# Rebuilding the instruction order of a one-core Conformer block: slack for GpSimd's results, shared last stores, and norm scaling of the tail on VectorE

## The chip, the cores and the metric

One core of a Trainium2 chip. The metric is the device time of one execution in microseconds (us), the median of the fast executions. The kernel before takes 951.6 us (three executions, 951.39 to 951.72). The profile of an execution covers a span about 1.8 us shorter than its time (949.6 for 951.43 before).

In this kernel TensorE (PE) multiplies matrices, VectorE (DVE) and ScalarE (ACT) work elementwise, GpSimd (POOL) takes the norms' powers and scalings and the edge copies, and SP issues most of the DMAs. "Clock" below is the share of full speed that TensorE was granted.

## The reference, cut to what matters

```python
B, T, D, K, H = 2, 4000, 144, 5, 4
h = layernorm(x);  x = x + 0.5 * (silu(h @ w_ff1a) @ w_ff1b)
h = layernorm(x);  q, k, v = split(h @ w_qkv)            # 4 heads of 36
x = x + softmax(q @ k.T * 36**-0.5) @ v @ w_o            # 4000 x 4000 scores a head
h = layernorm(x);  a, b = split(h @ w_pw1);  h = a * sigmoid(b)
c = depthwise_conv(h, dw)                                # 5 taps along T, zero padded
x = x + silu(c) @ w_pw2
h = layernorm(x);  x = x + 0.5 * (silu(h @ w_ff2a) @ w_ff2b)
return layernorm(x)
```

The 8000 tokens are handled as 16 chunks of 500. A chunk's convolution needs edge columns of its neighbours.

## The kernel before

The program is not written down in order. A scheduler runs while the kernel is built: threads (feed-forward, projections, attention, convolution of each chunk) ask for an engine and buffers, and a model with assumed costs decides whose instruction comes next. What it records is then replayed, with semaphores put in from the recorded reads and writes. So the chip runs a fixed order; if a result is later than the model assumed, an engine waits in that order (TensorE for 2.22 us at one place of the kernel before).

Model and records, cut:

```python
LAT = dict(pe=0.165, act=0.12, dve=0.083, pool=0.1, sp=2.0)     # us from an instruction's end to its result
def op(self, eng, name, *a, r=(), w=(), q=None, cost=0.1, kind=None, lat=None, **k):
    ...                                  # dependences from the keys in r and w
    self.free[eng] = o.t1 = start + cost
    o.done = start + cost + ((self.LAT[eng] if q is None else 2.0) if lat is None else lat)
```

Layer norm: VectorE takes the statistics, GpSimd the power -0.5. In the middle of the kernel GpSimd also scales; in the tail ACT or VectorE does:

```python
if not calm:                                              # the middle: GpSimd
    for j in range(n):
        op("pool", "tensor_scalar", XN[..., u, j, :], X[...], RS[..., 2, j], RS[..., 0, j], ..., cost=XN_COST, lat=XN_LAT)
elif mode["tail"] and R.free["act"] + XSLACK < R.free["dve"]:   # the tail, when ACT is free earlier
    op("dve", "scalar_tensor_tensor", ...)                # -mean * rstd
    for j in range(n):
        op("act", "activation", XN[...], X[...], ACT.Identity, bias=..., scale=..., cost=c_act(D))
else:
    for j in range(n):
        op("dve", "tensor_scalar", XN[...], X[...], ST[...], RS[...], ..., cost=0.231)
```

The edges of the convolution. U1 holds the gated values of 128 channels, U2 those of the other 16. Both copies write under one key, "UL", and the convolution over U1 reads that key:

```python
op("pool", "tensor_copy", U1[:, u, 2:4, 0:1], U1[:, up, 2:4, TB:TB + 1], r=[("U", up)], w=[("UL", u)], cost=0.25)
op("pool", "tensor_copy", U2[0:LP, u, 0:1], U2[0:LP, up, TB:TB + 1], r=[("V", up)], w=[("UL", u)], cost=0.25)
...
op("pe", "matmul", o[:, i0:i1, :], lhsT=DG[:, tap, :], rhs=U1[...], r=[("U", u), ("UL", u), ("UR", u), "DG"], w=[("ps", bk)], ...)
```

The softmax here doesn't subtract the row's maximum and nothing guards it: scores larger than these inputs give would overflow.

## Time and profile before

| stretch of the span (us) | length | ACT busy | ACT idle | VectorE busy |
|---|---|---|---|---|
| start, 0 to 139 | 139.0 | 121.8 | 17.2 | 121.2 |
| middle, 139 to the last exponential at 911.7 | 772.7 | 754.7 | 18.0 | 713.1 |
| tail, from there to the end | 37.9 | 23.4 | 14.5 | 21.6 |

ACT is the engine to watch: 804.0 of its 899.8 busy us are exponentials, and it is busy for 754.7 of the middle's 772.7 us, so an idle ACT there is counted as lost time. In the tail there are no exponentials, and the length is that of a chain of short steps on all engines. In lines of the trace a bracket holds the idle time just before an instruction and what ended it.

### The profile page before, as it was taken

How to read it: one execution, taken by the hardware profiler on the slowest of the kernel's cores; microseconds unless marked ns; L12 is line 12 of the kernel's file. 1: busy time of each engine (PE TensorE's matmuls, PEld its weight loads, DVE VectorE, ACT ScalarE, POOL GpSimd, SP SyncE). 2: the span in 40 equal slices, each digit the busy share in tenths (PEclk: the TensorE clock that was granted, in tenths of full speed). 3: DMA queues.
4: the chain of work that ended last, by engine and by line, in shares of the span. 5: the costliest groups of instructions: out<-in, count | busy, mean ns of one | idle time of the engine just before them, and what ended most of it. 6: DMA issues, size and time to landing. Idle time of an engine off the chain costs nothing.

```text
span 949.6 us, 26625 instructions
## 1 busy us (share of the span) xinstructions
PE 892.5 (94%) x11433; PEld 406.3 (43%) x11433; DVE 855.9 (90%) x1881; ACT 899.8 (95%) x1153; POOL 303.1 (32%) x524
## 2 busy tenths in 40 slices
PE   8999999999989999999999999999999999999996
PEld 6543434334444334444444343443444443434455
DVE  7998889999969999999899999999999998985874
ACT  5799998999979999999999999999999999999976
POOL 4130142410615215051322540232414343334052
PEclk9999999999989999999999999999999999999998
DMA  4000000000000000000000000000000000000000
GB/s 121 22 2 2 1 2 2 2 1 1 3 1 2 2 2 1 2 1 2 2 7 2 14 2 2 1 7 9 1 8 1 9 7 1 8 8 9 1 8 25
DMA packets 7321, 7.30 MB, mean 8 GB/s; under 512 B 2377, under 2 KB 7204, under 8 KB 7204
## 3 DMA queue, kind: packets, MB, share of 16 engines
q1 hardware_dynamic: 6046, 5.14, 1.8%
q8 instruction: 89, 1.46, 0.7%
q10 hardware_dynamic: 1158, 0.48, 0.2%
q14 instruction: 28, 0.23, 0.1%
HBM read 3.31 MB, written 2.30 MB: 6 GB/s over the span
## 4 chain that ended last, share of the span: by engine, by line
ACT 55%; PE 34%; DVE 8%; issue 1%; DMA 0%; POOL 0%; DVEq 0%
ACT PT L169 49%; PE PS L169 34%; ACT TH L169 5%; DVE PT L169 4%; DVE HT L169 1%; DVE ST L169 1%; ACT XN L169 1%; DVE X L169 1%; DMA X<-in_x_dram 0%; DVE XT L169 0%; DVE OTF L169 0%; DVE U L169 0%; ACT HT L169 0%; POOL U L169 0%; DVE XN L169 0%
## 5 line engine op out<-in xcount | busy, mean ns | idle before, releaser
L169 ACT ACTIVATE PT<-PS 128x1000 bf16<-128x1000 f32 (+1 forms) x869 | 804.0, 1046 | 16.1 <-PE PS L169 14.2
L169 PE MATMUL PS<-QT,KT 64*64 64x500 bf16 x3968 | 411.7, 385 | 27.8 <-ACT PT L169 20.2
L169 PE MATMUL PS<-PT,VA 64*37 64x500 bf16 x3968 | 361.0, 376 | 5.6 <-DVE OTF L169 2.7
L169 PEld LDWEIGHTS PS<-QT,KT 64*64 64x64 bf16 x3968 | 123.7, 104 | 221.6 <-ACT PT L169 144.3
L169 DVE TENSOR_SCALAR PT<-PS 128x500 uint16<-128x500 f32 x278 | 186.0, 670 | 15.4 <-PE PS L169 14.7
L169 DVE TENSOR_TENSOR PT<-PT 128x1000 f16<-128x1000 f16 (+1 forms) x278 | 187.6, 680 | 2.3
L169 POOL TENSOR_SCALAR RS<-ST 125x4 f32<-125x4 f32 x114 | 39.1, 343 | 427.3 <-DVE ST L169 421.7
L169 DVE TENSOR_SCALAR PT<-PT 128x1000 uint16<-128x1000 uint16 (+1 forms) x417 | 167.4, 417 | 2.6
L169 PEld LDWEIGHTS PS<-PT,VA 64*37 64x37 bf16 x3968 | 116.0, 95 | 116.9 <-issue 27.8
L169 POOL TENSOR_SCALAR XN<-X,RS 125x144 bf16<-125x144 bf16 x228 | 143.9, 643 | 5.9
L169 POOL TENSOR_TENSOR RS<-RS,NHALF 125x4 f32<-125x4 f32 (+2 forms) x101 | 99.5, 989 | 102.8 <-DVE RS L169 97.8
L169 ACT ACTIVATE TH<-PS 128x500 bf16<-128x500 f32 (+2 forms) x201 | 108.4, 562 | 8.4 <-PE PS L169 7.9
L169 DVE SCALAR_TENSOR_TENSOR HT<-TH,PS 128x500 bf16<-128x500 bf16 (+1 forms) x140 | 83.8, 615 | 12.9 <-ACT TH L169 12.7
L169 PE MATMUL PS<-XT,WA 72*128 72x500 bf16 (+2 forms) x280 | 73.8, 360 | 1.8 <-DVE HT L169 0.5
L169 DVE SCALAR_TENSOR_TENSOR X<-PS,X 125x288 bf16<-125x288 f32 x128 | 57.4, 452 | 10.7 <-PE PS L169 8.9
L169 DVE BATCH_NORM_STATS2 ST<-X 125x6 f32<-125x288 bf16 (+1 forms) x160 | 65.5, 447 | 1.4 <-DMA X<-in_x_dram 1.2
L169 PE MATMUL PS<-WB,HT 128*125 128x144 bf16 (+1 forms) x640 | 52.3, 230 | 1.7 <-DVE HT L169 1.4
L169 PEld LDWEIGHTS PS<-WB,HT 128*125 128x125 bf16 (+1 forms) x640 | 44.4, 136 | 15.5 <-issue 4.6
L169 POOL COPY U<-U 128x2 bf16<-128x2 bf16 (+1 forms) x54 | 17.1, 343 | 103.4 <-DVE U L169 103.4
L169 DVE COPY XT<-PS 72x1000 bf16<-72x1000 bf16 (+1 forms) x66 | 40.7, 617 | 7.6 <-PE PS L169 6.9
L169 PE MATMUL PS<-IDENT,XN 125*72 125x125 bf16 x512 | 42.6, 222 | 2.7 <-DVE XN L169 1.4
L169 PEld LDWEIGHTS PS<-IDENT,XN 125*72 125x72 bf16 x512 | 31.3, 113 | 23.2 <-issue 11.7
(88 smaller groups left out, 602.2 us busy)
## 6 DMA issues: line engine op xcount, KB each, us to landing
X<-in_x_dram SPq DMA_DIRECT2D x16, 140.6 KB
out_dram<-XN SPq DMA_DIRECT2D x13, 140.6 KB
out_dram<-XN SPq DMA_DIRECT2D x4, 70.3 KB
WA<-in_w_ff1a_dram ACTq DMA_DIRECT2D x1, 144.0 KB
WB<-in_w_ff1b_dram ACTq DMA_DIRECT2D x1, 144.0 KB, 2.7
WA<-in_w_ff2a_dram SPq DMA_DIRECT2D x1, 144.0 KB
WB<-in_w_ff2b_dram SPq DMA_DIRECT2D x1, 144.0 KB
out_dram<-XN SPq DMA_DIRECT2D x1, 139.5 KB
```

The costliest lines, as they stand in the source:

```text
L169: ins = getattr(eng, o.name)(*o.a, **o.k)
```

## The change

The policy tables are constants for each stage of the attention. DSLACK, for example, sets how far behind TensorE VectorE may be and still take a tile of exponentials off ACT.

The change's intent: leave room in the model for GpSimd's results, by assuming them later (norm scaling 0.1 to 0.6 us, edge copies 0.1 to 0.8); have the convolution ask for its edges before it is placed; retune the policy tables to the new model; in the tail, tell the model that a block scaled on ACT costs 0.41 us and prefer VectorE; let ACT issue some of the last stores.

```diff
-    BASE = dict(AHEAD=0.56, DSLACK=0.2, ..., BMIN=2.0, ...)
+    BASE = dict(AHEAD=0.56, DSLACK=0.4, ..., BMIN=1.6, ...)
     POLICY = {
-        "DSLACK": [0.2, 0.2, 0.2, 0.2, 0.2, 0.2, 0.2, 1.0, 1.0, 0.6, 0.2, ...],
+        "DSLACK": [0.4, 0.4, 1.5, 1.5, 1.5, 1.5, 1.5, 0.6, 1.0, 0.6, 0.4, ...],
  ... (DGAP, BMIN, SOON, EARLY retuned; LATE added; FDVE 4 to 5, PRELAG 0.5 to 0.7)
-                   ... w=[("XN", u)], cost=c_act(D))
+                   ... w=[("XN", u)], cost=0.41)
-    XSLACK = 0.0
+    XSLACK = 0.5
-    XN_LAT = 0.1
+    XN_LAT = 0.6
  ... (the four edge copies:)
-               cost=0.25)
+               cost=0.25, lat=0.8)
  ... (in post2, before the convolution's threads start:)
+        S.cur.ready = max([S.cur.ready] + [R.ready((k, c % NU), "pe") for k in ("U", "V", "UL", "UR")[:2 if e else 4]])
-        def put(dst, src, u, eng="sp"):
-            op(eng, "dma_start", dst, src, q=q, r=[("XN", u)], cost=0.7)
+        def put(dst, src, u):
+            act = mode["tail"] and R.free["act"] < R.free["sp"]
+            op("act" if act else "sp", "dma_start", dst, src, q=q, r=[("XN", u)], cost=0.4 if act else 0.7)
```

More of the change, by code (lines that the diff above doesn't have):

```diff
@@ L355, in bass_standalone__conformer_family_zipformer__speech_kernel @@
     NAN = 5
-    BASE = dict(AHEAD=0.56, DSLACK=0.2, DGAP=4.0, OFREE=1, OBATCH=1, LATE=0.3, BMIN=2.0, SOON=2, LIVE=3, MAXQ=3, EARLY=2)
+    BASE = dict(AHEAD=0.56, DSLACK=0.4, DGAP=4.0, OFREE=1, OBATCH=1, LATE=0.3, BMIN=1.6, SOON=2, LIVE=3, MAXQ=3, EARLY=2)
     POLICY = {
-        "DSLACK": [0.2, 0.2, 0.2, 0.2, 0.2, 0.2, 0.2, 1.0, 1.0, 0.6, 0.2, 0.2, 0.2, 0.2, 0.2, 0.2, 0.2, 0.2],
-        "DGAP": [4.0, 4.0, 4.0, 4.0, 4.0, 4.0, 4.0, 4.0, 4.0, 4.0, 4.0, 4.0, 4.5, 4.5, 4.0, 4.0, 4.0, 4.0],
+        "DSLACK": [0.4, 0.4, 1.5, 1.5, 1.5, 1.5, 1.5, 0.6, 1.0, 0.6, 0.4, 0.4, 0.4, 0.4, 0.4, 0.4, 0.4, 0.4],
+        "DGAP": [4.0, 4.0, 4.0, 4.0, 4.0, 4.0, 4.0, 4.0, 4.0, 4.5, 4.5, 4.5, 4.5, 4.5, 4.0, 4.0, 4.0, 3.5],
         "OFREE": [1, 1, 1, 1, 1, 1, 1, 1, 1, 1, 1, 3, 1, 3, 0, 0, 0, 1],
         "OBATCH": [1, 1, 1, 1, 1, 1, 1, 1, 1, 1, 1, 1, 1, 0, 1, 1, 1, 2],
-        "BMIN": [2.0, 2.0, 2.0, 2.0, 1.8, 1.8, 1.8, 2.0, 2.0, 1.6, 2.0, 3.5, 2.0, 2.0, 2.0, 2.0, 2.0, 1.8],
-        "SOON": [2, 2, 2, 2, 2, 2, 2, 2, 2, 2, 2, 2, 2, 2, 2, 2, 5, 3],
+        "LATE": [0.3, 0.3, 0.3, 0.1, 0.1, 0.3, 0.3, 0.3, 0.3, 0.3, 0.3, 0.3, 0.3, 0.3, 0.3, 0.3, 0.3, 0.3],
+        "BMIN": [1.6, 1.6, 1.6, 1.6, 1.8, 1.6, 1.8, 1.6, 1.6, 1.6, 1.6, 3.5, 3.5, 1.6, 1.6, 1.6, 1.6, 1.8],
+        "SOON": [2, 2, 2, 2, 2, 2, 2, 2, 2, 2, 2, 2, 2, 4, 4, 2, 5, 3],
         "LIVE": [3, 2, 2, 2, 3, 3, 3, 3, 3, 2, 2, 3, 3, 3, 2, 3, 3, 3],
         "MAXQ": [3, 3, 3, 3, 3, 3, 3, 3, 2, 2, 2, 2, 2, 3, 3, 3, 3, 3],
-        "EARLY": [2, 2, 2, 2, 2, 2, 2, 1, 1, 1, 1, 1, 1, 2, 2, 2, 2, 2],
+        "EARLY": [2, 2, 2, 2, 2, 2, 2, 1, 1, 2, 2, 2, 2, 2, 2, 2, 2, 2],
     }
@@ L376, in bass_standalone__conformer_family_zipformer__speech_kernel @@
     NQ = 2
-    FDVE = 4
+    FDVE = 5
     FEQ = 2
     HALF = 5
-    PRELAG = 0.5
+    PRELAG = 0.7
     BEND = 2.0
@@ L621, in ln @@
                    bias=RS[0:rows, u, 2, j:j + 1], scale=RS[0:rows, u, 0, j:j + 1],
-                   r=[("X", c, b0 + j), ("NM", u), ("RS", u)] + xe, w=[("XN", u)], cost=c_act(D))
+                   r=[("X", c, b0 + j), ("NM", u), ("RS", u)] + xe, w=[("XN", u)], cost=0.41)
         else:
@@ L966, in halo @@
             op("pool", "tensor_copy", U1[:, u, 2:4, 0:1], U1[:, up, 2:4, TB:TB + 1], r=[("U", up)], w=[("UL", u)],
-               cost=0.25)
+               cost=0.25, lat=0.8)
             op("pool", "tensor_copy", U2[0:LP, u, 0:1], U2[0:LP, up, TB:TB + 1], r=[("V", up)], w=[("UL", u)],
-               cost=0.25)
+               cost=0.25, lat=0.8)
         if cc == CPB - 1 or c == NCH - 2:
@@ L1017, in post1 @@
             op("pool", "tensor_copy", U1[:, up, 0:2, TB + 1:TB + 2], U1[:, u, 0:2, 1:2], r=[("U", u)],
-               w=[("UR", up)], cost=0.25)
+               w=[("UR", up)], cost=0.25, lat=0.8)
             op("pool", "tensor_copy", U2[0:LP, up, TB + 1:TB + 2], U2[0:LP, u, 1:2], r=[("V", u)], w=[("UR", up)],
-               cost=0.25)
+               cost=0.25, lat=0.8)
         glu_done.add(c)
@@ L1138, in store @@
             if e and 3 in bs:
-                put(out_tok[c - 1][TB - 1:TB, 2:4, :], XN[TB:TB + 1, u, 0:2, :], u, "act")
+                put(out_tok[c - 1][TB - 1:TB, 2:4, :], XN[TB:TB + 1, u, 0:2, :], u)
             xnp.give(u)
```

## The prediction

> **What bounds the kernel now.** I read the page from the top: busy shares first, then the chain that ended last, then the groups, then waits and timelines of the places that stood out.
>
> ```profile
> PE 892.5 (94%) x11433; PEld 406.3 (43%) x11433; DVE 855.9 (90%) x1881; ACT 899.8 (95%) x1153; POOL 303.1 (32%) x524
> ...
> PEclk9999999999989999999999999999999999999998
> ...
> ACT 55%; PE 34%; DVE 8%; issue 1%; DMA 0%; POOL 0%; DVEq 0%
> ...
> L169 ACT ACTIVATE PT<-PS 128x1000 bf16<-128x1000 f32 (+1 forms) x869 | 804.0, 1046 | 16.1 <-PE PS L169 14.2
> ```
>
> ACT is busy for 95% of the span and the chain runs mostly on it: the exponentials of the attention scores are 804 of its 899.8 us. So time can only be won in three ways: less work for ACT, fewer holes in ACT's row, or a shorter end after the last exponential. The clock row has one digit that is not 9 in the middle, and that is the first thing to chase. To place holes I cut the span at two points: 139, where the two programs stop being the same (below), and 911.7, where ACT's last exponential ends. The sums by stretch, in the order PE, weight loads, DVE, ACT, POOL:
>
> ```profile
> 0.00:139.00 139.00, 132.26 (x1680) 65.67 (x1680) 121.23 (x335) 121.75 (x171) 39.47 (x70) 1.00 0.09 26
> 139.00:911.70 772.70, 733.19 (x9426) 317.93 (x9424) 713.14 (x1476) 754.71 (x930) 253.12 (x436) 1.00 0.02 4
> 911.70:949.60 37.90, 27.10 (x333) 22.70 (x330) 21.57 (x73) 23.38 (x55) 10.50 (x20) 0.92 0.06 16
> ```
>
> In the middle ACT is idle for 772.7 - 754.7 = 18.0 us. The narrower stretch 264 to 284 has 12.99 us of ACT busy in 20.00, so 7.0 of the 18.0 us lie in that one place. Its timeline and the windows of 2 us around it:
>
> ```profile
> 264.97 1.25 DVE L169 TENSOR_TENSOR PT<-PT 128x1000 uint16<-128x1000 uint16 x2
> 266.14 0.74 DVE L169 TENSOR_SCALAR PT<-PT 128x1000 uint16<-128x1000 uint16 x2
> ```
>
> ```profile
> 264.52 2.66 POOL L169 COPY U<-U 80x1 bf16<-80x1 bf16 x3 [2.03 <-DVE U L169]
> ...
> 266.98 0.39 PE L169 MATMUL PS<-U,DG 128*128 128x500 bf16 x1 [2.22 <-POOL U L169]
> ```
>
> ```profile
> 268.00:270.00 2.00, 2.00 (x10) 0.56 (x8) 0.00 (x0) 1.81 (x2) 0.00 (x0) 0.50 0.00 0
> 270.00:272.00 2.00, 2.00 (x13) 0.54 (x13) 0.00 (x0) 1.58 (x2) 0.00 (x0) 0.50 0.00 0
> 272.00:274.00 2.00, 2.00 (x21) 1.06 (x23) 0.87 (x2) 0.75 (x2) 0.00 (x0) 0.50 0.00 0
> ```
>
> The convolution's first matmul waits 2.22 us for edge columns that GpSimd copies. A copy of one column usually takes about 0.19 us (median of the 54 such copies, 187 ns); the first of these three took 2.41 us and ended at 266.93, just after DVE's run of work (264.38 to 266.88) ended. Then TensorE's clock stands at half for 6.8 us (267.5 to 274.4), so scores come late and ACT starves until about 282. One late 80x1 copy costs 7 us.
>
> [...] In this trace a store's issue is about 0.27 us on SP, so sharing stores can save a few tenths.
>
> **The change, part by part.** This kernel decides its order while it is built, from assumed costs. The change makes GpSimd's results appear later in that model (norm scaling 0.1 to 0.6, edge copies to 0.8), makes the convolution ask for its edges before it is placed, retunes the policy tables, makes ACT's norm scaling in the tail look dearer, and lets ACT issue stores in the tail. Comparing the two built programs:
>
> First, the start is the same: up to TensorE instruction 1680, ACT 179, VectorE 336. In the trace TensorE's lies at 139.0 us, so the 139 us stay.
>
> Second, ACT's work in the middle: 2 fewer 1000-column exponentials (2 x 1.054 = 2.1 us less), 2 more 500-column tanh (2 x 0.645) and one small one (0.29), together 0.5 us less: 754.2. VectorE gets two more attention tiles (about 4.0 us each from the rows: 2 x 0.67, 3 x 0.417, 2 x 0.68) and some feed-forward and convolution products, about 9 us more: 722. In some 765 us that is 94%, below ACT's 98.6%.
>
> Third, the edge stall. I counted the TensorE columns that stand between the last left-over GLU matmul (the one that the U edge depends on) and the next convolution. Before, the smallest distance is 9,000 columns, and it is exactly the stall at 267; the next, 14,000 and 17,000, did not stall. After, the smallest is 21,000. So I expect no convolution to wait for GpSimd by over half a microsecond, and no half clock in the middle: 7.0 us won, all on the path, as ACT is the bound.
>
> Fourth, the other 11.0 us of ACT holes. The largest is 2.49 us at 162.87, where TensorE runs about 18,000 columns of other work within 8 score matmuls. The new order has such a place too (about 21,800 columns), and otherwise similar densities. I give the new order 10 us of holes, so 8.0 us won of 18.0.
>
> Fifth, the tail, 37.9 us, a chain in which ACT is busy only 23.4. Norm scaling on ACT falls from 22 blocks to 10, on VectorE it rises from 6 to 22. A block costs 0.50 on ACT and 0.31 on VectorE, and ACT's form needs a further 0.15 us VectorE instruction. The last stretch is clearest:
>
> ```profile
> 942.56 0.69 POOL L169 TENSOR_TENSOR RS<-RS,NHALF 126x2 f32<-126x2 f32 x1 [0.37 <-DVE RS L169]
> 942.58 3.29 ACT L169 ACTIVATE XN<-X,RS 125x144 bf16<-125x144 bf16 x8 [0.90 <-DVE RS L169]
> 943.29 0.16 DVE L169 SCALAR_TENSOR_TENSOR RS<-ST,RS 126x2 f32<-126x2 f32 x1 [0.67 <-POOL RS L169]
> ```
>
> The last power ends at 943.25, but ten scalings queue on ACT until 945.87. With the last two on VectorE (0.6 us) that point is near 943.9: 2.0 us won. The two earlier norms of the last chunk win about 0.5 each. Fewer feed-forward tiles with tanh and one whole convolution are also left after the last exponential (three fewer VectorE products of 0.67 us, 15 fewer convolution matmuls), and a second issuer saves about 0.3. Overlaps eat some of this; I take 3.5 us in all.
>
> Sum: 951.6 - 0.5 - 8.0 - 3.5 = **939.6 us**, 1.3% less.
>
> **Rivals.** (a) The bound moves to VectorE: its middle rises to 94%[...] and TensorE waits elsewhere. For it: the early chunks' policy now allows many more tiles. Against it: only 2 tiles more in all, and waits of TensorE for GpSimd's norm output were 1.4 us in total before. It would take back 3 to 6 us: 943 to 946. (b) Order noise: a rebuilt order makes a new hole like the one at 162.87 or, if TensorE stands for 2 us, another half-clock stretch of 7 us; the cluster of 21,800 columns is the candidate. Then 944 to 948. (c) The order is better everywhere: holes fall to 5 us and the tail to 33: about 933. With no holes at all in the middle and a tail of 34.4, 139 + 754.2 + 34.4 and 1.8 us of difference between time and span give 929.4, so a gain over 2% (below 932.6) needs holes below about 3 us. (d) Stores bound the end, so the shorter chain gains nothing: against it, the last packet lands 2.6 us after the last issue and the queue is nearly empty before.
>
> **Range and chances.** The two sure terms (edge stall, last scalings) give 9 us. The rest is order luck of about 6 us either way: 933 to 947. Over 2% faster is barely above the floor: 0.07. Over 2% slower would need 30 us of new holes: 0.01. Within 2%: 0.92.
>
> **What would show it.** Right: the clock row is whole in the middle, no TensorE wait for POOL U over 0.5 us, ACT's busy total near 893, ACT idle in the middle near 10, the span after the last exponential near 34.5. Wrong: a second half-clock stretch, a new wait of TensorE for POOL XN or of ACT for scores over 3 us, VectorE waits vanishing at a busy share above 96% in the middle, or a tail as long as before although scaling moved.

The 0.3 us for a second issuer, within the 3.5, is the estimate from what a store's issue takes on SP in the trace of before (median 0.26 us of 19, 0.25 to 0.32); the "2 us" and "7 us" of rival (b) are this trace's one case, 2.22 us of waiting with 6.8 us of half clock.

## The result, and the profile after

The changed kernel takes 938.9 us (four executions, 938.82 to 939.81) against 951.5 us for the kernel before on the same chip. The ratio is 0.9874, 95% interval 0.9856 to 0.9891: a gain clear of noise, and within the 2% that counts as "same". A ratio here is the mean time of one kernel's fast executions over that of the other's of the same rounds, so not quite the ratio of the medians quoted. Executions over 1.5% slower than the fastest of the same kernel are left out of the means.

The page after, in the order of the lines shown of before: busy time, clock by slice, the chain, the exponentials' group.

```profile
PE 891.4 (95%) x11427; PEld 405.4 (43%) x11427; DVE 864.1 (92%) x1905; ACT 893.2 (95%) x1141; POOL 291.9 (31%) x518
...
PEclk9999999999999999999999999999999999999999
...
ACT 50%; PE 32%; DVE 14%; POOL 2%; issue 1%; DMA 0%; POOLq 0%; DVEq 0%
...
L169 ACT ACTIVATE PT<-PS 128x1000 bf16<-128x1000 f32 (+1 forms) x867 | 801.7, 1046 | 13.8 <-PE PS L169 12.4
```

ACT works 6.6 us less, and no slice of the clock falls below 9. The sums by stretch (length, then busy time of PE, weight loads, DVE, ACT, POOL; clock; DMA), cut at the same two events:

```profile
0.00:139.00 139.00, 133.07 (x1679) 66.51 (x1679) 121.19 (x334) 121.73 (x171) 39.45 (x70) 1.00 0.09 26
139.00:904.66 765.66, 733.56 (x9430) 316.89 (x9428) 719.07 (x1490) 752.67 (x930) 242.26 (x431) 1.00 0.01 4
904.66:937.02 32.36, 24.75 (x324) 21.96 (x321) 23.80 (x82) 18.85 (x41) 10.22 (x17) 0.97 0.08 24
```

The start is the same. The middle is 7.0 us shorter: 2.0 by less work on ACT, 5.0 by less idling (18.0 to 13.0). The tail is 5.5 us shorter. TensorE's waits in the middle, totals with count and longest:

```profile
PE PS L169 <- ACT PT L169: 20.8, 51, 0.8
PE PS L169 <- POOL XN L169: 1.6, 2, 1.1
PE PS L169 <- DVE OTF L169: 1.4, 3, 0.8
```

The wait for POOL U is gone. Two small waits for GpSimd's norms (POOL XN) are new. The largest hole on ACT is now the 2.46 us that end at 433.73, behind a dense group of other matmuls:

```profile
431.00 0.27 ACT L169 ACTIVATE TH<-PS 80x125 bf16<-80x125 f32 x1 [1.34 <-PE PS L169]
...
433.73 2.90 ACT L169 ACTIVATE PT<-PS 128x1000 bf16<-128x1000 f32 x3 [2.46 <-PE PS L169]
```

The end of the tail: the last power on GpSimd ends at 933.29, VectorE scales the last blocks until 933.87, and two stores go out on each of SP and ACT.

```profile
931.93 1.36 POOL L169 TENSOR_TENSOR RS<-RS,NHALF 126x2 f32<-126x2 f32 x2 [0.73 <-DVE RS L169]
932.24 0.17 DVE L169 TENSOR_SCALAR RS<-ST 125x2 f32<-125x2 f32 x1
932.66 1.21 DVE L169 TENSOR_SCALAR XN<-X,ST,RS 126x144 bf16<-126x144 bf16 x4 [0.25 <-POOL RS L169]
932.67 0.79 SPq L169 DMA_DIRECT2D out_dram<-XN  x2
933.24 0.95 ACTq L169 DMA_DIRECT2D out_dram<-XN  x2
```

Before, eight scalings in a row (942.58 to 945.87) kept ACT busy 2.6 us past the last power; now it is 0.6 us.

### The profile page after: what moved, and what is told of

The parts are those of the page before. It is cut to its first block, busy times and chain, and to the rows that moved or that the text cites. A ratio compares the mean times of both kernels' runs of the same rounds, so it can differ in the third digit from the quotient of the medians.

```text
span 937.0 us, 26616 instructions
## 1 busy us (share of the span) xinstructions
PE 891.4 (95%) x11427; PEld 405.4 (43%) x11427; DVE 864.1 (92%) x1905; ACT 893.2 (95%) x1141; POOL 291.9 (31%) x518
## 4 chain that ended last, share of the span: by engine, by line
ACT 50%; PE 32%; DVE 14%; POOL 2%; issue 1%; DMA 0%; POOLq 0%; DVEq 0%
ACT PT L169 44%; PE PS L169 32%; DVE PT L169 8%; ACT TH L169 5%; DVE ST L169 1%; DVE HT L169 1%; POOL XN L169 1%; DVE X L169 1%; POOL RS L169 1%; DVE XT L169 1%; DVE OTF L169 1%; DMA X<-in_x_dram 0%; DVE AN L169 0%; DVE KT L169 0%; DVE XN L169 0%
## 5 line engine op out<-in xcount | busy, mean ns | idle before, releaser
L169 DVE TENSOR_SCALAR PT<-PS 128x500 uint16<-128x500 f32 x282 | 188.8, 671 | 11.9 <-PE PS L169 11.2
L169 DVE TENSOR_TENSOR PT<-PT 128x1000 uint16<-128x1000 uint16 (+1 forms) x282 | 190.1, 679 | 1.7
L169 DVE TENSOR_SCALAR PT<-PT 128x1000 uint16<-128x1000 uint16 (+1 forms) x423 | 169.9, 418 | 2.3
L169 POOL TENSOR_SCALAR XN<-X,RS 125x144 bf16<-125x144 bf16 x224 | 135.3, 616 | 5.8
L169 DVE SCALAR_TENSOR_TENSOR X<-PS,X 125x288 bf16<-125x288 f32 (+1 forms) x128 | 57.2, 452 | 11.5 <-PE PS L169 9.6
L169 DVE BATCH_NORM_STATS2 ST<-X 125x6 f32<-125x288 bf16 x160 | 65.6, 447 | 1.4 <-DMA X<-in_x_dram 1.3
```

Source lines behind the costliest of these rows:

```text
L169: ins = getattr(eng, o.name)(*o.a, **o.k)
```

## The experiments

A rebuilt order changes everything at once, so the first five runs leave the order of the middle as it was and repair one thing in it. Runs 6 to 10 add or take back the slack and the tail's rules and let the scheduler rebuild the order; runs 11 and 12 search further. All twelve gave correct results.

**1. The late copy, without a new order.** After the order is fixed, the matmuls of the convolution over U1 lose their wait for the edge copies of U2, which they do not read; the wait came from the shared key "UL". No data that is read is left unguarded.

```diff
+    for o in R.ops:
+        if o.eng == "pe" and o.name == "matmul" and o.k["lhsT"].tensor.name == "DG":
+            o.deps = [(d, raw) for d, raw in o.deps
+                      if not (d.eng == "pool" and d.name == "tensor_copy" and d.a[0].tensor.name == "U2")]
```

> The kernel before with its instruction order untouched; only the wait of the convolution over U1 for the edge copies of U2 (a tensor it does not read) is taken out. Theory (the late 2.41 us copy, the 2.22 us hole on TensorE and the half clock after it cost 7.0 us of ACT idle): 951.5 - 6.5 = 945, clock whole in the middle, ACT idle between 264 and 284 near 0.5 us, all else as before. Rival (order: another wait ends at the same place, or the time won is given back a little later because TensorE or VectorE is as full as ACT): 949 or more.

Measured: 946.4 us (three fast executions, 946.33 to 946.41) against 951.3, so 4.9 us. The stall is real, but taking it away is worth 4.9 and not the expected 6.5. The profiled execution (mean clock 0.751, 1052.7 us) is not used; run 5 has the same middle at full clock.

**2. The hole or the clock?** TensorE still waits for the copy but works meanwhile on matmuls whose result is overwritten.

```diff
+    fill = [36 matmuls of 128 columns into the stalled convolution's own bank]
+    R.ops[at:at] = fill        # ahead of the convolution's first matmul, which has start=True
```

> The kernel before with 36 throw-away 128-column matmuls put ahead of the stalled convolution, in its own bank: TensorE still waits for GpSimd's copy, but works meanwhile, so its clock should not fall. Theory (most of the 7 us is the half clock that follows the hole, not the hole): 951.5 - 4.5 = 947, with the wait's own 2 us hole on ACT left and no half-clock stretch. Rival (the 2.2 us hole itself and the catching up cost it all): 951 to 951.5. If the clock falls all the same, idle time is not what lowers it.

Measured: 948.6 us (948.62 to 948.83). The clock stays whole (1.00 below, where it was 0.50), and the wait stays (the three copies start at 264.74 and take 2.66 us, the convolution starts at 267.21). Windows of 2 us (busy of PE, weight loads, DVE, ACT, POOL; clock):

```profile
268.00:270.00 2.00, 2.00 (x20) 0.72 (x18) 0.00 (x0) 2.00 (x3) 0.00 (x0) 1.00 0.00 0
270.00:272.00 2.00, 2.00 (x33) 0.98 (x33) 0.23 (x1) 1.88 (x4) 0.00 (x0) 1.00 0.03 8
```

These are the windows that stood at 0.50 in the kernel before; TensorE completes 20 and 33 matmuls in them in place of 10 and 13. So the half clock costs 951.3 - 948.6 = 2.7 us and the wait itself 948.6 - 946.4 = 2.2 us. The expected 4.5 for the clock was too much, but neither is zero. The ratio alone, 0.9982 (0.9960 to 1.0004), would not show the 2.7: its kernel before mixes two kinds of executions.

The 28 executions of the kernel before that ran beside the experiments say the same by themselves: 6 took 948.2 to 948.6 us at a mean clock of 0.997 to 0.998, 2 took about 950.0, and 20 took 951.2 to 952.9 at 0.992 to 0.995. The six lie within 0.6 us of run 2. In run 1, whose order has no such wait, the three fast executions lie within 0.1 us. In the six the clock evidently did not fall; their traces were not taken.

**3. The tail's rules alone.** The kernel before with these lines of the change; nothing differs up to the last exponential.

```diff
-    XSLACK = 0.0   ...  cost=c_act(D)
+    XSLACK = 0.5   ...  cost=0.41
+    (stores shared as in the change)
```

> The kernel before with only the tail's rules of the change (ACT's norm scaling dearer and 0.5 us of slack, stores shared by two issuers); the order up to the last exponential is the same. Theory (norm scaling on VectorE shortens the chain: last scalings 2.0 us, earlier norms about 0.5 us each): 951.5 - 2.5 = 949, tail 37.9 to 35.4 us. Rival 1 (the tail rules give all of the 5.5 us that the changed kernel's tail won): 946. Rival 2 (the tail hangs on its matmul chain and the last store, so nothing): 951 to 951.5.

Measured: 948.3 us (946.93 to 949.63; the stall is still in it, and the ratio's interval reaches 1.0002). The tail tells it more exactly: the last exponential ends at 911.8, as before, and the span at 946.6, so the tail is 34.8 in place of 37.9: 3.1 us. Theory, with a slightly larger size; not the whole 5.5.

**4. The shared stores alone.**

```diff
-            op(eng, "dma_start", dst, src, q=q, r=[("XN", u)], cost=0.7)
+            act = mode["tail"] and R.free["act"] < R.free["sp"]
+            op("act" if act else "sp", "dma_start", dst, src, q=q, r=[("XN", u)], cost=0.4 if act else 0.7)
```

> The kernel before with only the sharing of the tail's stores between SP and ACT. Theory[...]: 951.2, within 0.5 us of before. Rival (stores queue on SP and hold the end): 950 or less.

The theory's 951.2 is the estimate from the 0.26 us of a store's issue.

Measured: 950.7 us (948.52 to 951.69), ratio 0.9996, interval 0.9966 to 1.0026; in the profile the tail is 37.8. With the norm scaling as before, sharing is worth nothing that this can resolve, so run 3's gain is the scaling's, alone or together with the sharing; the scaling without the sharing was not run.

**5. Both repairs, the middle not reordered.** The edits of runs 1 and 3 together.

> The kernel before with both repairs and nothing reordered in the middle: the convolution no longer waits for the U2 edge copies, and the tail's rules of the change. Theory (the two gains lie in different stretches and add): 951.3 - 4.9 - 3.0 = 943.4, and repeated runs within 0.3 us of each other, as no half clock falls in the middle. Rival (they overlap): 945 or more. The 4 to 5 us to the changed kernel's 938.9 would then belong to the retuned order.

Measured: 943.4 us (943.26 to 943.67), as the sum said; the four lie within 0.41 us, not 0.3. The trace shows why the copy no longer matters: it is as late as ever, and the convolution starts beside it.

```profile
264.76 2.66 POOL L169 COPY U<-U 80x1 bf16<-80x1 bf16 x3 [2.04 <-DVE U L169]
264.95 0.39 PE L169 MATMUL PS<-U,DG 128*128 128x500 bf16 x1
```

The sums of 264 to 284 (columns as above) in this kernel and, below, in the kernel before:

```profile
264.00:284.00 20.00, 19.13 (x247) 9.69 (x245) 16.17 (x37) 17.50 (x24) 7.33 (x13) 1.00 0.01 2
```

```profile
264.00:284.00 20.00, 17.04 (x181) 7.58 (x180) 11.41 (x24) 12.99 (x18) 3.43 (x5) 0.83 0.00 1
```

Even without the stall ACT idles 2.5 of these 20 us. The stall's own share of the 7.0 us of idling is 4.5, near the 4.9 that run 1 won.

**6. The slack alone, order rebuilt.** The kernel before with the lines of the change for XN_LAT, the four edge copies and the convolution's question; policy and tail as before.

```diff
-    XN_LAT = 0.1                 # and cost=0.25 at the four edge copies
+    XN_LAT = 0.6                 # and cost=0.25, lat=0.8; and the S.cur.ready line
```

> The kernel before with only the slack for GpSimd in the model (norm scaling 0.6, edge copies 0.8, the convolution asks for its edges), no policy table and no tail rule changed. Theory (the slack is what takes the stall away): no TensorE wait for POOL U above 0.5 us, middle about 5 us shorter: 946. Rival (a rebuilt order is luck: without retuning, new holes eat it): 948 to 952.

Measured: 948.3 us (947.53 to 949.06), between theory and rival. The stall is gone (no TensorE wait for POOL U over 0.15 us, mean clock 0.999 in the profiled execution), but the middle is 772.5 us, as long as before: ACT got 2.3 us more work there (757.0), and a hole of 2.57 us came up at 380.6. What the slack won in the middle, the rebuilt order gave back; the 3 us come from a shorter tail (34.5). By times alone they are not clear of noise (interval of the ratio 0.9954 to 1.0005).

**7. The change without the slack.**

```diff
-    XN_LAT = 0.6                 # lat=0.8 at the copies, S.cur.ready line
+    XN_LAT = 0.1                 # none of these
```

> The changed kernel without the slack for GpSimd, its policy tables and tail rules kept. The smallest distance between left-over GLU and convolution is 19,000 columns in it, so if the stall is a matter of that distance it does not come back. Theory (distance decides, and here the tables alone give it): 939 to 941, no TensorE wait for POOL U over 0.5 us. Rival (the slack itself is needed): a stall and half clock return, 944 or more.

Measured: 945.3 us (944.65 to 947.2). Here my theory fell. No convolution waits, but the same thing happens at another place, with the norm scaling: GpSimd's four blocks take 5.55 us, and TensorE's transposes wait for them.

```profile
820.92 5.55 POOL L169 TENSOR_SCALAR XN<-X,RS 125x144 bf16<-125x144 bf16 x4
...
826.52 0.63 PE L169 MATMUL PS<-IDENT,XN 125*72 125x125 bf16 x8 [2.15 <-POOL XN L169]
```

```profile
828.00:830.00 2.00, 2.00 (x18) 0.30 (x10) 1.90 (x5) 2.00 (x3) 1.90 (x4) 0.50 0.00 0
830.00:832.00 2.00, 2.00 (x17) 1.08 (x14) 1.49 (x2) 1.12 (x2) 1.69 (x4) 0.50 0.00 0
```

A 2.15 us wait, then half clock for 6.8 us. The distance of convolutions from their edges was one case: another result of GpSimd that TensorE needs can stall it too.

The stall is not all of the 6.4 us that this run loses to the change. The profiled execution is the slowest of the four (947.2). The one whose mean clock was 0.999, so evidently without half clock, still took 944.65. ACT's largest hole is elsewhere, 4.12 us up to 381.4, behind another dense group of matmuls (about 18,900 columns, counted from the trace). Runs 9 and 10 ask which slack matters.

**8. The change with the tail's rules of before.**

```diff
-    XSLACK = 0.5   ...  cost=0.41   ...  stores shared
+    XSLACK = 0.0   ...  cost=c_act(D)   ...  stores on SP, one on ACT
```

> The changed kernel with the tail's rules of before (cheap norm scaling on ACT, stores on SP), the same order up to the last exponential. Theory (tail rules are worth the same 3.0 us here as in the kernel before): 938.9 + 3.0 = 941.9. Rival (in the new order less work is left after the last exponential, so the rules matter less): 939.5 to 940.5.

Measured: 940.8 us (940.62 to 940.93), so the rules are worth 1.9 us in the new order, between theory and rival. The tail is 34.0 against 32.4, and 37.9 in the kernel before. So of the tail's 5.5 us some 3.9 come even without its rules: in the new order fewer pieces are left after the last exponential (one VectorE product of the feed-forward with tanh in place of four, the first of them under way at the cut; one convolution less).

**9 and 10. Which slack.** The change with one of the two taken back.

```diff
  9:  -    XN_LAT = 0.6           10:  -  cost=0.25, lat=0.8 (four copies), S.cur.ready line
      +    XN_LAT = 0.1                +  cost=0.25
```

> The changed kernel with the slack for the edge copies kept and the slack for GpSimd's norm scaling taken back (0.6 to 0.1). Theory (in the new order the norm scaling is what would stall TensorE, as in the run without any slack: a 2.15 us wait for POOL XN at 826 and half clock after it): a TensorE wait for POOL XN of over 1.5 us with half clock again, 943 to 946. Rival (the edge slack is what counts): 939 to 941.

> The changed kernel with the slack for the norm scaling kept and that for the edge copies (and the convolution's own question for its edges) taken back. Theory (norm slack is what counts in the new order; the convolutions stay far enough from their edges, smallest distance 16,000 columns): no half clock in the middle, 939 to 942. Rival (both are needed): a TensorE wait for POOL U over 1.5 us with half clock, 944 or more.

Measured: 950.7 us (950.33 to 953.17) with the edge slack alone, above the 943 to 946 expected, and 941.6 us (941.36 to 941.81) with the norm slack alone, as expected. Run 9 has the wait again:

```profile
PE PS L169 <- POOL XN L169: 2.9, 3, 2.1
```

and its mean clock is 0.994 in the profiled execution, where the change has 0.999. But of the 11.8 us that it loses to the change, the stall can explain no more than the middle's part (770.5 against 765.7, with the 4.12 us hole of run 7 in it); the larger part is its tail, 38.9 us against 32.4. Run 10 has a mean clock of 0.998 to 1.000 and a middle of 764.5 us, 1 us shorter than the change's; it loses in the tail (36.5), where 379 TensorE matmuls are left in place of 324. So with these tables, a 2 us wait for a norm scaling with a lower mean clock in the profiled execution (0.996 in run 7, 0.994 in run 9) came in both orders built without the norm slack and in neither order built with it (0.999 in the change, 0.998 in run 10). That is less than it looks: every run here rebuilds the order, runs 7 and 9 stall at the same scaling, and the tables were tuned with the slack in the model. Tables tuned without it were not run. The slack for the edges comes with another 2.7 us, by way of the tail and not by a stall avoided; why that tail comes out better was not taken apart, and it may be the order's luck.

**11 and 12. Further tables.** A random search over the policy tables and a few constants under the kernel's own assumed costs, with all slack kept; two of its results were run.

```diff
-        "DSLACK": [0.4, 0.4, 1.5, 1.5, 1.5, 1.5, 1.5, 0.6, ...],  ENDS = 1.6, DRAIN = 0.75
+ 11:    "DSLACK": [0.2, 0.2, 1.5, 1.5, 1.0, 0.4, 1.0, 1.0, ...],  ENDS = 2.0, DRAIN = 0.6,  ... (all tables)
+ 12:    "DSLACK": [1.5, 1.5, 1.0, 1.5, 0.6, 0.6, 0.4, 1.0, ...],  ENDS = 2.0, DRAIN = 0.7,  ... (all tables)
```

> The changed kernel with policy tables from a further random search under the kernel's own assumed costs, all slack kept. In its order the dense cluster of 21,760 columns (the changed kernel's largest ACT hole, 3.8 us around 431 to 434) is gone, and the smallest distance between left-over GLU and convolution is 16,000 columns. Theory (what is left are order holes, and the slack makes the assumed costs good enough to search on): 935 to 938, no half clock in the middle. Rival (the order is already at the point where luck on the chip decides): 939 to 943, with a wait for POOL XN or a new cluster.

> As the other tuned kernel, from another start of the search: fewest exponentials on ACT (850), the cluster of 21,760 columns still there. Theory (2 fewer exponentials and an earlier last exponential): 936 to 938.5. Rival (VectorE, two more tiles, or luck): 939 to 943.

Measured: 937.9 us (936.44 to 939.07) and 938.5 us (938.35 to 938.68), against the change's 938.9 in other rounds. The ratios to before, 0.9867 and 0.9870, lie inside the interval of the change's 0.9874, so neither is shown to be faster, though both times are what their theories said. The profiled execution of run 11 took 936.4 us; its cluster hole is gone (ACT idle in the middle 10.3 us), but waits for POOL XN came in its place:

```profile
PE PS L169 <- POOL XN L169: 4.0, 3, 1.9
```

Run 12 has three such waits too (3.4 us in all). Its last exponential ends 2.1 us earlier than the change's (902.6), but its tail is 34.1 us. An order searched under an assumed 0.6 us still makes TensorE wait up to 1.9 us for a scaling. More of the slack, not more search, would be the next thing to try; no run here shows it.

## Why the prediction was right

The time, 938.9 against 939.6 forecast, is right, and the parts that carry it are the right ones; three of its terms were off in size and their errors cancel. That the total comes within 0.7 us is luck; that both large terms, the stall and the tail, are gains is not.

**The start** is the same, as said (TensorE's instruction 1680, counted from 0, at 139.09 and 139.03).

**Second, ACT's work in the middle:** 2.0 us less in place of 0.5. The exponentials were counted right (1000-column group 795.8 to 793.5 us over the kernel), but the added tanh cost less than their mean durations: over the kernel the 500-column group has one instruction more and 0.9 us less (88.2 to 87.3). In the trace of before, ACT's instructions can overlap (a tanh starts at 910.61, while the exponential before it is shown until 910.75), so their durations here do not simply add.

**Third, the edge stall:** that it goes, and that the distance in TensorE columns shows it, is right for this order. "7.0 us won, all on the path" is the step that was mis-sized: run 1 measured 4.9, of which 2.7 is half clock and 2.2 the wait. The 7.0 was all of ACT's idling in a window of 20 us, and run 5 shows 2.5 of it with no stall there. And the criterion was too narrow: run 7, with distances of 19,000 and more, stalls on a norm scaling instead.

**Fourth, the other holes:** 10 us forecast for the new order, 13.0 measured. The named candidate is the largest: the cluster of 21,800 columns begins at TensorE's instruction 5279 (426.9 us), and ACT is idle for 1.34 and 2.46 us up to 433.7.

**Fifth, the tail:** 5.5 us in place of 3.5. The scaling's 2.0 us at the end is there (0.6 us after the last power in place of 2.6; the prediction read ten queued scalings, the row has eight), runs 3 and 8 give the rules 3.1 and 1.9 us, and run 4 gives the second issuer nothing, where 0.3 was assumed. What was undersized is the work moved ahead of the last exponential: run 8's tail, with the old rules in the new order, is already 3.9 us shorter.

The sum by terms: forecast 0.5 + 8.0 + 3.5 = 12.0; measured 2.0 + 5.0 + 5.5 = 12.5 in the spans. By experiments: the stall 4.9 and the tail's rules 3.0 give 943.4 (run 5) without a new order; the reordering gives the last 4.5, of which 1.8 is ACT work in the middle (754.5 to 752.7) and 2.4 tail (34.8 to 32.4).

**Rivals.** (a) VectorE did rise (713 to 719 us in the middle, 94%), but GpSimd's norm scalings did not get longer (mean 643 to 616 ns), and the two new waits for POOL XN sum to 1.6 us. (b) the cluster hole came, a second half-clock stretch did not. (c) came in the tail (32.4, where it said 33) and not in the holes (13.0, where it said 5). (d) did not happen: the shorter chain shortened the tail.

## What to carry to other kernels

When an order is fixed before the run, a small result that comes late can cost far more than its own time (here a copy that usually takes 0.19 us, and took 2.41, cost 4.9): give such results room in the model, for every consumer and not only for the one that stalled last, look afterwards whether the room was enough (run 11 still waits 1.9 us), and check what an instruction waits for against what it reads. Size a stall by taking it away, not by all the idling around it. And when a rebuilt order changes everything at once, repair the old order by hand first: here that showed that 8 of the 12.5 us needed no new order.

## What the traces show of half clock and of GpSimd's small operations

- Visible TensorE holes of 2.22 us (before) and 2.15 us (run 7) came with half clock. It lasted 6.83 us before (267.53 to 274.35) and 6.8 us in run 7 (0.50 from 828 to 834, 0.79 from 834 to 836), with TensorE busy in the windows shown. The lag differed: half clock began 0.5 us after the hole's end before and 1.5 us after it in run 7. Run 11's profiled execution, with a hole of 1.9 us, had no such stretch (mean clock 0.999), and in six executions of the kernel before the clock evidently did not fall (0.997 to 0.998). In run 2, where TensorE worked through the first of these holes, the clock stayed at 1.00. Beyond this, what decides it was not shown. One execution of run 1, on one core, ran at 0.75 nearly throughout and took 1052.7 us in place of 946.4. What else ran on the chip then is not known.
- The one-column copy took 2.41 us, while VectorE's instructions beside it took 0.41 to 0.68 us each. It started at 264.52 (starts on GpSimd are rough) and ended at 266.93, 0.05 us after the last of them. What held it was not shown: no run took VectorE's work away there.
- What the case turns on is the spread of a small GpSimd operation. In the kernel before, with VectorE busy for 90% of the span, the edge copies took 0.18 to 2.41 us and the norm scalings 0.45 to 2.96 us a block; after, with VectorE at 92%, 0.18 to 1.50 and 0.45 to 2.73 us.
